# Start-up of a four-layer attention kernel: blank fills on VectorE, later weights loaded after the first rows, and a re-planned order

## The chip, the cores and the metric

The kernel runs on one core of one Trainium2 chip. The metric is the device time of one execution in microseconds (us); the median of seven executions is compared. Of the engines, PE is TensorE (matrix products), ACT is ScalarE, DVE is VectorE, POOL is GpSimd, and SP is SyncE, which here only issues DMA transfers. "PEld" are TensorE's weight loads.

## What is computed

Two kinds of layer alternate, A, B, A, B, over 2048 rows of 512 values, each added to its input:

```python
x = x + _A_ref(_layernorm(x, axis=-1), A_wqkv, A_wo)
x = x + _B_ref(_layernorm(x, axis=-1), B_wq, B_wk, B_wv, B_wo)
x = x + _A_ref(_layernorm(x, axis=-1), A_wqkv, A_wo)
x = x + _B_ref(_layernorm(x, axis=-1), B_wq, B_wk, B_wv, B_wo)
```

Layer A projects to q, k and v (32 heads of 16 values); each row attends to eight rows of its head, itself and every second one before it (offsets 0, 2, ..., 14), where they exist. Layer B has 32 query heads of 16 values on one shared k and v, and every row attends to all 2048 rows:

```python
scores = jnp.einsum("bhqd,bkd->bhqk", q, k) * (Dh ** -0.5)
p = _softmax(scores, axis=-1)
o = jnp.einsum("bhqk,bkd->bhqd", p, v)
```

## The kernel before

**Tiling.** The rows are split by parity and taken in four chunks of 512 rows (four tiles of 128). `chunk(l, c, ...)` does one chunk of a layer A: `ln` normalises, `qkv` projects, `unit` does banded attention, `a_out` projects back, and `b_in` normalises again and makes q, k and v of the following layer B. Layer B's attention is a stream of score tiles (`Stream`): a tile's exponential is either made on ScalarE, two tiles in one instruction (`pt`, L1486), or in a 16-bit approximation on VectorE (`t`, L1490) with a pass over four tiles on VectorE (`i`, L1500) and one on GpSimd (`i`, L1495). Such a tile costs three matmuls with the values, a ScalarE tile one (all `o`, L1512). Scores (`st`, `dv`, L1471) use a quarter of the array's rows each, and value products a quarter of its columns, so four of either run at once.

**What sets the order.** Nearly all instructions are emitted by a planner, `Sched`. Every piece of work is an `op` with a list of engines and assumed durations, its dependencies, a priority `prio` and an earliest start `after` (ns). The planner repeatedly takes the earliest candidate, weighs it by these constants, and writes down a fixed order for each engine; `chain` then ties each engine's instructions to that order. Each engine runs its list strictly in order. `SLACK`, `PATIENCE` and the table `BIAS` steer when the stream's scores are let in between other matmuls and which of the two ways a tile takes. Where the plan leaves TensorE idle, `keep_awake` adds idle matmuls against `zeros` (`stir`, L1079), reckoned at 108 ns for 256 columns; they go to a free bank of PSUM (named `stir` in the profile), or add zero to an open accumulation (`o<-zeros`). At the very start 46 such matmuls of 512 columns are emitted by hand.

**The start.** The work ahead of the planner is not ordered by it. SP loads x in five pieces (L1802: two of 256 KB, three of 512 KB), ScalarE's queue issues the four pieces of the q, k, v weights `w_sb` (L1806). Then SP issues `woA` (8 DMAs, the weights of the A output), `wq_sb` (4), `wk_sb`, `wv_sb` (one each) and `woB` (4), the weights of layer B. GpSimd builds the small constants: the identity, the band mask's pattern (L889 to L895, made into bits by VectorE at L898), `halves`, `off`, `kmask` (L320 to L324) and `sel` (L1831). After these it clears what must be zero or one: the check buffers (L850), the padding in the v tiles of both buffer sets (`v`, `lb`, `KAB`, L988), all of `k` (L989), `P` (L991), `vs` (L992), and layer B's value padding by `pad_v` (L1096 to L1098).

**The first rows.** `ln` takes statistics on VectorE (L1156), combines them (L1162), lets GpSimd work out scale and shift in four small instructions (L1166 to L1169), for rows 0, 1 and then 2, 3 in the first two chunks, and normalises on any of three engines (L1184, L1187). In these two chunks TensorE transposes the result (`pT`, L1198); in others a DMA does. Then come the projections (L1135).

Of the kernel before, what the change touches and what calls it, by code (L numbers as in the profile page):

```python
# [435 lines left out]
SLACK, PATIENCE = 1158.8, 464.8  # L436
# [180 lines left out]
class Stream:  # L617

    GROUP = 4
    BIAS = {"act": -72.8, "act2": 4311.9, "vec": 438.1, "pv": 169.4, "pv_in": 209.6, "batch": 19, "few": 15.0,  # L620
            "copy": 1.4, "pass": 284.2, "lag": -654.7, "both": 628.5, "next": 1451.0, "late": 32.5, "open": 55.9,
            "close": 6.0}
# [216 lines left out]
class Checks:  # L839
# [4 lines left out]
    def __init__(self, nc, pool):  # L844
        self.nc, self.pool = nc, pool
        self.a = pool.tile([128, 256], F32, name="chk_a")
        self.b = pool.tile([128, 2, 32], F32, name="chk_b")
        self.t = None
        for x in (self.a, self.b):
            nc.gpsimd.memset(x[:], 0.0)  # L850
# [36 lines left out]
def build_band_mask(nc, cpool):  # L887
# [10 lines left out]
    nc.vector.tensor_scalar(out=bits[:].bitcast(I16), in0=m[:], scalar1=-1.0, scalar2=None, op0=ALU.mult)  # L898
# [42 lines left out]
class Net:  # L941

    PRIO, LATER = 0.0, -201.0

    def __init__(self, ctx, tc, w, S, nlayers, out_view):
        self.tc, self.nc, self.w, self.out_view = tc, tc.nc, w, out_view
        nc = tc.nc
# [38 lines left out]
        for k2 in range(4):  # L986
            for B in self.sets:
                nc.gpsimd.memset(B.vpair(k2)[:, :, :, :, DH:2 * DH], 0.0)  # L988
        nc.gpsimd.memset(self.k.t[:], 0.0)  # L989
        for b in self.P.bufs:  # L990
            nc.gpsimd.memset(b.t[:], 0.0)  # L991
        nc.gpsimd.memset(self.vs.t[:, :, :, DH:2 * DH], 0.0)  # L992
        self.pad_v(0)
# [15 lines left out]
        self.tail, self.first_pass = {}, {}  # L1009
# [83 lines left out]
    def pad_v(self, l):  # L1093
        va, vd = self.va[l], self.vd[l]
        g = self.nc.gpsimd
        out = [g.memset(va[:, :, 17:32], 0.0), g.memset(va[:, :, 16:17], 1.0), g.memset(vd[:, :, :, 17:32], 0.0)]  # L1096
        for j in range(NJ):
            out.append(g.memset(vd[:, :, j, 16:17], J_W[j]))  # L1098
        return out
# [25 lines left out]
    def mm_full(self, pairs, deps, name):  # L1125
# [17 lines left out]
        b = self.op("pe", half * MM, rest, behind=[a], solid=True, prio=-1760.9 + self.PRIO)  # L1143
# [3 lines left out]
    def ln(self, B, src, deps, after=(0.0,) * 4, quick=False, own=None):  # L1147
# [6 lines left out]
        for i in range(4):  # L1154
            def emit(op, i=i):
                self.chain("dve", nc.vector.bn_stats(out=stats[:, i, :], in_=src(i)))  # L1156

            st.append(sm.used(self.op("dve", 596.0, emit, [*deps[i], *sm.prev], prio=-73.4 + self.PRIO, after=after[i])))
# [13 lines left out]
        for some in ((0, 1), (2, 3)) if quick else ((0, 1, 2, 3),):  # L1172
            ag = sm.used(self.op("dve", 70.0 * len(some), lambda op, some=some: aggr(op, some), [st[i] for i in some],
                                 prio=-1530.5 + self.PRIO))
            ag = sm.used(self.op("pool", 1700.0, lambda op, some=some: scalars(op, some), [ag], prio=10.4 + self.PRIO))
            nm.update(dict.fromkeys(some, ag))
        B.xnT.renew()
        xnT, done = B.xnT.t, []
        for i in range(4):
            xn = ring.next()  # L1180

            def norm(op, i=i, xn=xn):
# [3 lines left out]
                else:  # L1186
# [5 lines left out]
                                        prio=146.4 + self.PRIO, port=("pool",))))  # L1192
            cols = xnT[:, :, i * 128:(i + 1) * 128]
            if quick:
                def turn(op, xn=xn):
                    pT = self.psum(op, [128, 4, 128], BF16, "pT")
                    for ft in range(4):
# [4 lines left out]
                                     prio=-1811.6 + self.PRIO))  # L1202
                tr = self.op({"act": act_ns(512), "dve": 400.0}, 0, lambda op, cols=cols, tr=tr: self.chain(
                    op.eng, (nc.scalar.copy if op.eng == "act" else nc.vector.tensor_copy)(
                        out=cols, in_=self.y.pop(tr)[:])), [tr], frees=[tr], prio=125.9 + self.PRIO)
            else:
                tr = xn.used(self.op("sp", 1300.0, lambda op, cols=cols, xn=xn: self.chain(
                    "sp", nc.sync.dma_start_transpose(out=cols, in_=xn.t[:])), [n, *B.xnT.prev], prio=-2414.9 + self.PRIO))
# [9 lines left out]
    def chunk(self, l, c, deps):  # L1218
# [5 lines left out]
        after = ((7300.0, 7300.0, 8800.0, 8800.0) if c == 0 else (9000.0 + 2500.0 * c,) * 4) if first else (0.0,) * 4  # L1224
# [33 lines left out]
    def qkv(self, B, c, xops, quick):  # L1258
# [20 lines left out]
        def split(op):  # L1279
            for g in range(4):  # L1280
                for h in range(2):
# [5 lines left out]
        k = kp if quick else [[B.k.used(B.oncA.used(self.op("sp", 8 * DMA, split, [*kp, *B.k.prev],  # L1287
                                                                  prio=-248.9 + self.PRIO)))]] * 4
# [3 lines left out]
        for k2 in range(4):  # L1292
# [13 lines left out]
            m0 = self.op("pe", 450.0, mm, xops + vb.prev, want=("bank", "aux"), solid=True, mode="h64", prio=1077.4 + self.PRIO)  # L1306
            m = self.op("pe", 450.0, lambda op, mm=mm: mm(op, i=1), behind=[m0], solid=True, mode="h64", prio=-515.0 + self.PRIO)
# [21 lines left out]
    def unit(self, B, c, t, kd, qkv):  # L1329
# [14 lines left out]
        for gh in range(2):  # L1344
            def score(op, gh=gh):
                st = self.st[op] = self.slot[op.buf].tile([128, 2, 512], F32, name="st")
                for col, w, kx, _, q0 in parts:
                    for j in range(2):
# [7 lines left out]
                         solid=True, mode="row", prio=-259.7 + self.PRIO)  # L1356
            exps.append(P.used(self.op("act", act_ns(2 * ncol), lambda op, gh=gh, sc=sc: self.chain(
                "act", nc.scalar.activation(out=P.t[:, gh, :, c0:UC], in_=self.st.pop(sc)[:, :, c0:UC], func=AF.Exp,  # L1358
                                            scale=DH ** -0.5)), [sc], frees=[sc], prio=-46.0 + self.PRIO)))
# [8 lines left out]
        ms = P.used(self.op("dve", 800.0, mask, exps, prio=-532.6 + self.PRIO, port=("dve",)))  # L1368
# [16 lines left out]
        def dn(op):  # L1385
            o = state["o"]
            for gh in range(2):
                for q0, q1, b1 in ((SPILL, NQ, 0), (0, SPILL, 0 if over else 1)):
                    for j in range(2):
# [9 lines left out]
                     prio=193.1 + self.PRIO, want=("bank", "aux"))  # L1399
        p1 = self.op("pe", 165.0, lambda op: pv(op, 1), behind=[p0], solid=True, mode="c64", prio=-2353.3 + self.PRIO)  # L1400
        m = self.op("pe", 250.0, dn, behind=[p1], solid=True, mode="c64", prio=-1347.9 + self.PRIO)
        m.lend = p0
        for x in (p0, p1, m):
# [5 lines left out]
            out=lg.t[:], in_=state["o"][:, 1, :], func=AF.Ln)), [m, *lg.prev], prio=-177.0 + self.PRIO))  # L1409
        ex = lg.used(rc.used(self.op("act", act_ns(256), lambda op: self.chain("act", nc.scalar.activation(  # L1410
            out=rc.t[:], in_=lg.t[:], func=AF.Exp, scale=-1.0)), [ln, *rc.prev], prio=-60.7 + self.PRIO)))
        if t == 0 and kd == 0:
# [3 lines left out]
            [ex, *B.oncA.prev], frees=[m], prio=-246.0 + self.PRIO)))  # L1416
# [6 lines left out]
        lg.used(self.op("pool", 1400.0, see, [ex], prio=1614.3, port=("pool",)))  # L1423
        return on

    def a_out(self, B, l, c, units):
        nc, adds = self.nc, []
        for qi in range(4):
# [7 lines left out]
                prio=-22.5 + self.PRIO))  # L1436
        return adds

    def b_in(self, B, l, c, adds):
# [3 lines left out]
        m = self.proj(B, lambda kt: w.wkR[:, kt, :], xops, "kb")  # L1443
# [14 lines left out]
        v = B.xnT.used(self.op("pe", 400.0, mm, xops + self.padded[l], want=("bank", "aux"), solid=True, prio=209.4 + self.PRIO))  # L1458
# [56 lines left out]
    def close(self, n, bank, when):  # L1515
# [15 lines left out]
        e = X.used(self.op("dve", 599.0, evac, X.prev if fresh else list(X.cur), after=when, frees=[held], prio=-214.6))  # L1531
# [7 lines left out]
    def rows(self, l, qc, t, a, evac):  # L1539
# [43 lines left out]
        r = R2.used(S2.used(self.op("dve", 260.0, recip, [m, self.ready[l, qc, t, 0], *R2.prev], prio=-175.2)))  # L1583
        R2.used(S2.used(self.op("pool", 620.0, see, [r], prio=178.2)))
        d = R2.used(self.op("sp", 2 * DMA, to_dram, [r]))
        b = lb.used(self.op("sp", DMA, spread, [d, *lb.prev]))
        if t == 0:
            self.oncB.renew()
        self.ready[l, qc, t] = self.oncB.used(lb.used(X0.used(
            self.op("pool", 1300.0, scale, [b, m, *self.oncB.prev], prio=1009.5, port=("pool",)))))  # L1590
# [7 lines left out]
    def out_rows(self, l, qc, qi):  # L1598
        m = self.oncB.used(self.mm_full([(self.oncB.t[:, t, qi * 128:(qi + 1) * 128], self.w.woB[:, t, :])
                                         for t in range(4)], [self.ready[l, qc, t] for t in range(4)], "y"))  # L1600
        return self.op("dve", 599.0, lambda op: self.add_y(l, qc, qi, self.y.pop(m)[:]), [m], frees=[m], prio=-57.3)

    def retire_w(self):
# [7 lines left out]
        z = self.op("pool", 960.0, lambda op: self.chain("pool", nc.gpsimd.memset(w.woP, 0.0)), done, prio=661.6)  # L1611

        def load(op):
            for g in range(4):
# [5 lines left out]
                             self.oncA.cur, prio=4790.1)  # L1620
# [14 lines left out]
    def close_tail(self, a, evac):  # L1635
# [6 lines left out]
        for cs in parts:  # L1642
# [7 lines left out]
            dns.append(self.op("pe", 4 * MM * n / 512, mm, [evac], want=("bank", "aux"), solid=True, prio=FIRST))  # L1650
# [54 lines left out]

    def run(self):
        self.padded = {0: []}
        adds = []
        for c in range(self.NQC):
            adds += self.chunk(0, c, [[]] * 4)  # L1710

        def pad(op):
            for l in range(1, self.NB):
                for i in self.pad_v(l):
                    self.chain("pool", i)

        self.padded[1] = [self.op("pool", 1500.0, pad, adds, prio=-258.1)]
        warm = self.bank[0].tile([128, 512], F32, name="stir", tag="bk")
        for _ in range(46):
# [48 lines left out]
def kernel(  # L1768
# [30 lines left out]
    last = None  # L1799
    pieces = [(0, 2), (2, 2), (4, 4), (8, 4), (12, 4)]  # L1800
    for n, (t0, k) in enumerate(pieces):
        i = nc.sync.dma_start(out=x_bf[:, t0:t0 + k, :], in_=xv[t0 // 8, :, t0 % 8:t0 % 8 + k, :])  # L1802
        order_after(tc, i, last)
        last = i
        if n < 4:
            nc.scalar.dma_start(out=w.w_sb[:, n, :], in_=wqv[:, n, :])  # L1806
    w.zeros = cpool.tile([128, 128], BF16, name="zeros")
    nc.vector.memset(w.zeros[:], 0.0)  # L1808
    w.ident = build_ident(nc, cpool)
    w.nhalf = cpool.tile([128, 4], F32, name="nhalf")  # L1810
    nc.gpsimd.memset(w.nhalf[:], -0.5)
    w.band = build_band_mask(nc, cpool)
    w.halves = build_halves(nc, cpool)
    w.off = {j: cpool.tile([128, 4], I32, name=f"off{j}") for j in (1, 2)}
    for j in (1, 2):
        nc.gpsimd.memset(w.off[j][:].bitcast(I16), round(J_OFF[j]))
    nc.scalar.preload_act_table_set("natural_log_exp_and_others")
    wov = A_wo.rearrange("(t h g d) n -> g h d t n", t=4, h=2, g=4, d=DH)
    for g in range(4):
        for h in range(2):  # L1820
            nc.sync.dma_start(out=w.woA[32 * g + 16 * h:32 * g + 16 * h + 16, :, :], in_=wov[g, h])
    w.wq_sb = load_w(nc, cpool, B_wq, "wq_sb", D, (nc.sync,))
    bconsts = build_consts_B(nc, cpool, B_wk, B_wv)
    w.wv_sb, w.wkR, w.kmask = bconsts
    w.woB = load_w(nc, cpool, B_wo, "woB_sb", D, (nc.sync,))
    w.wo_dram = B_wo
    w.kscale = fpool.tile([128, 2], F32, name="kscale")
    nc.vector.tensor_scalar(out=w.kscale[:], in0=w.kmask[:], scalar1=K_SCALE, scalar2=None, op0=ALU.mult)

    w.sel = fpool.tile([128, 128], F32, name="sel")  # L1830
    nc.gpsimd.memset(w.sel[:], 1.0)  # L1831
    nc.gpsimd.affine_select(out=w.sel[:].rearrange("p (g r) -> p g r", r=32), in_=w.sel[:].rearrange(
        "p (g r) -> p g r", r=32), compare_op=ALU.is_equal, fill=0.0, base=-16, pattern=[[-32, 4], [0, 32]],
        channel_multiplier=1)
# [38 lines left out]
```

## Time and profile before

| | us |
|---|---|
| seven runs, median (lowest to highest) | 1540.32 (1536.35 to 1546.76) |
| the profiled execution, its own time | 1546.78 |
| its span in the trace | 1545.1 |
| busy in the span: PE / ACT / DVE / POOL | 1493.1 / 1449.1 / 1341.1 / 889.4 |
| first 16 us: busy PE / DVE / ACT / POOL | 12.60 / 8.67 / 1.28 / 14.44 |
| mean granted TensorE clock over the span | 0.977 |

A timeline line of the profile reads: start, time covered, engine, line of the program, operation, what is written from what, shape, count; in square brackets the engine's idle time before it and what ended it. A matmul row that is long is not PE at its peak, since matmuls are pipelined. The chain of waits is the path of work followed back from the last instruction, each step to what released it. The granted clock is the share of TensorE's full clock.

The profiled execution's own time is 1.7 us more than its span. Changes are worked out against it and then set against the median, which is 6.5 us lower.

### The profile page before, as it was taken

Reading aid. Unit: us, or ns where it says so; the run is one execution under the profiler, and the core shown is the slowest. Engines: PE = TensorE matmul, PEld = TensorE weight load, DVE = VectorE, ACT = ScalarE, POOL = GpSimd, SP = SyncE. Lnnn points to the kernel's source line nnn. Section 1 sums busy time; section 2 is a strip of 40 time slices with the busy share of each in tenths; the row PEclk is TensorE's granted clock in tenths of the full one; section 3 lists DMA queues with packets and bytes.
Section 4 is the critical chain, followed back from the end, with each engine's and each line's share of the span. In section 5 each row is a group of like instructions: output and inputs, shape, how many; then the busy total and the mean of one; then the engine's idle time right before and its main releaser. Section 6 shows DMA issues by size and latency. Waiting matters only on the chain.

```text
span 1545.1 us, 42500 instructions
## 1 busy us (share of the span) xinstructions
PE 1493.1 (97%) x17361; PEld 519.1 (34%) x17361; DVE 1341.1 (87%) x2261; ACT 1449.1 (94%) x1769; POOL 889.4 (58%) x749
## 2 busy tenths in 40 slices
PE   8999999999999999999999999999999999999997
PEld 3544334322333224323243233422332223223322
DVE  5585875899689996999879997899999999999996
ACT  4788997899999998999999999999999999999995
POOL 5553633566465654656565664756666656665664
PEclk8999996999999999999999999999999999999998
DMA  4001110011110011100111001001000000000000
GB/s 137 4 15 16 16 29 3 15 39 27 22 21 19 13 22 21 27 13 13 25 20 23 13 13 28 3 19 38 26 13 13 13 26 13 13 13 29 15 13 16
DMA packets 84114, 32.95 MB, mean 21 GB/s; under 512 B 71688, under 2 KB 77448, under 8 KB 83912
## 3 DMA queue, kind: packets, MB, share of 16 engines
q1 hardware_dynamic: 83048, 28.33, 8.6%
q8 instruction: 138, 2.26, 0.6%
q10 hardware_dynamic: 864, 1.84, 0.3%
q14 instruction: 64, 0.52, 0.1%
HBM read 13.53 MB, written 2.61 MB: 10 GB/s over the span
## 4 chain that ended last, share of the span: by engine, by line
PE 61%; ACT 27%; issue 5%; DVE 4%; POOL 1%; SPq 1%; DMA 1%; ACTq 0%; DVEq 0%; POOLq 0%
ACT pt L1486 24%; PE o L1512 23%; PE st L1471 19%; PE y L1135 3%; PE stir L1079 2%; PE qb L1135 2%; PE k L1135 2%; PE q L1135 2%; PE v L1302 2%; DVE t L1490 2%; PE dv L1471 2%; ACT P L1358 1%; PE st L1351 1%; PE oa L1378 1%; SPq L1283 1%
## 5 line engine op out<-in xcount | busy, mean ns | idle before, releaser
L1486 ACT ACTIVATE pt<-st 128x1024 bf16<-128x1024 f32 x1368 | 1281.3, 1151 | 22.6 <-PE dv L1471 9.5
L1495 POOL TENSOR_TENSOR i<-t,off 128x1024 int32<-128x1024 int32 (+1 forms) x341 | 643.2, 1886 | 512.3 <-DVE i L1500 304.6
L1490 DVE TENSOR_SCALAR t<-dv 128x512 int16<-128x512 f32 x1360 | 868.9, 684 | 51.3 <-PE dv L1471 42.5
L1471 PE MATMUL st<-QT,KAB 32*128 32x512 bf16 x1403 | 276.9, 386 | 7.4 <-ACT pt L1486 4.9
L1512 PE MATMUL o<-pt,region 128*32 128x512 bf16 x1333 | 270.6, 388 | 0.6 <-DVE x_sb L1434 0.6
L1471 PE MATMUL st<-QT,region 32*128 32x512 bf16 x1333 | 261.2, 381 | 10.1 <-ACT pt L1486 7.1
L1512 PE MATMUL o<-pt,VEa 128*32 128x512 bf16 x1403 | 266.9, 392 | 0.6 <-ACT pt L1486 0.2
L1512 PE MATMUL o<-i,region 128*32 128x512 f16 x1430 | 254.7, 387 | 0.6 <-DVE i L1500 0.4
L1500 DVE TENSOR_SCALAR i<-t 128x2048 int16<-128x2048 int16 (+1 forms) x341 | 239.1, 701 | 0.5
L1512 PE MATMUL o<-i,VEd 128*32 128x512 f16 x1290 | 232.3, 390 | 0.8 <-POOL i L1495 0.7
L1471 PE MATMUL dv<-QT,region 32*128 32x512 bf16 x715 | 230.2, 385 | 0.8 <-DVE t L1490 0.6
L1471 PE MATMUL dv<-QT,KAB 32*128 32x512 bf16 x645 | 204.3, 386 | 0.7 <-DVE t L1490 0.7
L1512 PE MATMUL o<-t,region 128*32 128x512 f16 x715 | 187.4, 387 | 0.0
L1471 PEld LDWEIGHTS <-KAB 32*128 32x128 bf16 x2048 | 90.7, 91 | 267.6 <-issue 263.3
L1471 PEld LDWEIGHTS <-region 32*128 32x128 bf16 x2048 | 93.1, 91 | 260.2 <-issue 257.2
L1512 PE MATMUL o<-t,VEd 128*32 128x512 f16 x645 | 167.1, 388 | 0.0
L1512 PEld LDWEIGHTS <-region 128*32 128x32 f16 (+1 forms) x3478 | 77.9, 94 | 162.2 <-issue 157.9
L1358 ACT ACTIVATE P<-st 128x576 bf16<-128x576 f32 (+1 forms) x128 | 88.8, 717 | 5.9 <-PE st L1351 4.1
L1512 PEld LDWEIGHTS <-VEd 128*32 128x32 f16 x1935 | 66.8, 94 | 74.6 <-issue 69.9
L1512 PEld LDWEIGHTS <-VEa 128*32 128x32 bf16 x1403 | 59.8, 94 | 82.3 <-issue 80.3
L1365 DVE TENSOR_TENSOR P<-P,bandmask 128x576 int32<-128x576 int32 x64 | 54.8, 858 | 30.9 <-ACT P L1358 28.6
L1079 PE MATMUL stir<-zeros 32*128 32x256 bf16 (+11 forms) x267 | 72.3, 300 | 8.5 <-DVE zeros L1808 1.1
(176 smaller groups left out, 1245.3 us busy)
## 6 DMA issues: line engine op xcount, KB each, us to landing
lb<-rd SPq DMA_DIRECT2D x31, 256.0 KB
X<-X SPq DMA_DIRECT2D x124, 32.0 KB
k<-oncA SPq DMA_DIRECT2D x48, 64.0 KB
w_sb<-in_A_wqkv_dram ACTq DMA_DIRECT2D x4, 384.0 KB
region<-in_A_x_dram SPq DMA_DIRECT2D x3, 512.0 KB
out_dram<-w_sb SPq DMA_DIRECT2D x3, 512.0 KB
S<-X SPq DMA_DIRECT2D x62, 8.0 KB
rd<-R SPq DMA_DIRECT2D x62, 8.0 KB
```

Source lines behind the costliest of these rows:

```text
L1079: self.chain("pe", self.nc.tensor.matmul(out[0:m, 0:n], lhsT=z[0:k, 0:m], rhs=z[0:k, 0:1].to_broadcast([k, n]), start=start, stop=start, t ...
L1135: self.chain("pe", self.nc.tensor.matmul(st["ps"][:], lhsT=lhsT, rhs=rhs, start=first and n == 0, stop=last and n == len(some) - 1))
L1283: self.chain("sp", nc.sync.dma_start(out=B.k.t[r, :, :, h, :], in_=B.oncA.t[r].rearrange("p t (b i) -> p t b i", i=64)))
L1302: self.chain("pe", nc.tensor.matmul(ps[0][64 * a:64 * a + 64, i], lhsT=B.xnT.t[:, kt, kb * 64:(kb + 1) * 64], rhs=wv[:, kt, a, :, :], star ...
L1358: "act", nc.scalar.activation(out=P.t[:, gh, :, c0:UC], in_=self.st.pop(sc)[:, :, c0:UC], func=AF.Exp, scale=DH ** -0.5)), [sc], frees=[sc ...
L1365: self.chain("dve", nc.vector.tensor_tensor(out=x, in0=x, in1=self.w.band[:].unsqueeze(1).to_broadcast([128, 16, NQ // 2]), op=ALU.bitwise ...
L1471: self.chain("pe", self.nc.tensor.matmul(out, lhsT=self.KAB[l][32 * g:32 * g + 32, a, kt * 128:(kt + 1) * 128], rhs=self.QT[32 * g:32 * g ...
L1486: self.chain("act", self.nc.scalar.activation(out=self.pt[pt][:, 0:n, :], in_=self.st.pop(key)[:, 0:n, :], func=AF.Exp, scale=E_SCALE))
L1490: self.chain("dve", self.nc.vector.tensor_scalar(out=self.t[buf][:, r, :].bitcast(I16), in0=self.dv[bank][:], scalar1=-U_BIAS, scalar2=U_B ...
L1495: i = self.nc.gpsimd.tensor_tensor(out=self.i[out][:, 0:n, :].bitcast(I32), in0=self.t[buf][:, 0:n, :].bitcast(I32), in1=self.w.off[j][:, ...
L1500: i = self.nc.vector.tensor_scalar(out=self.i[out][:, 0:n, :].bitcast(I16), in0=self.t[buf][:, 0:n, :].bitcast(I16), scalar1=J_OFF[j], sca ...
L1512: self.chain("pe", self.nc.tensor.matmul(self.o[bank][32 * g:32 * g + 32, :], lhsT=lhsT, rhs=rhs, start=first, stop=last, tile_position=(0 ...
```

## The change

Fills: `Checks`, `Net.__init__` and `pad_v(0)` clear on VectorE in place of GpSimd, before the first statistics, in the order check buffers, P, v padding, vs, layer B's value padding. `k` is not cleared any more. `kmask` is made on VectorE, `kscale` straight after it; the band mask's bits are made on GpSimd. `nhalf` comes ahead of the identity on GpSimd.

Loads: only the first three x pieces are issued at once. `late_loads` gives the planner a one-element VectorE memset (earliest 8400 ns) that writes into `woA`, and SP's remaining 20 DMAs wait for it: `woA`, `wq_sb`, `wk_sb`, `wv_sb`, the last two x pieces, `woB`. `wkR` (VectorE) and `sel` (GpSimd) are planned from 26,000 and 30,000 ns.

Plan: the planner is told that VectorE, GpSimd and TensorE are free at 4500, 4000 and 8300 ns; 17 idle matmuls instead of 46 open TensorE; the earliest starts of the first statistics move from 7300 and 8800 to 4800 and 7100 ns; `SLACK`, `PATIENCE`, `BIAS` and most priorities get new values (a few are shown), so that the order of all engines differs through the whole run.

```diff
-SLACK, PATIENCE = 1158.8, 464.8
+SLACK, PATIENCE = 658.9, 588.4
-    BIAS = {"act": -72.8, "act2": 4311.9, "vec": 438.1, "pv": 169.4, "pv_in": 209.6, "batch": 19, "few": 15.0,
-            "copy": 1.4, "pass": 284.2, "lag": -654.7, "both": 628.5, "next": 1451.0, "late": 32.5, "open": 55.9,
-            "close": 6.0}
+    BIAS = {"act": -51.1, "act2": 3433.0, "vec": 438.1, "pv": 169.4, "pv_in": 208.5, "batch": 22, "few": 15.0,
+            "copy": 1.8, "pass": 108.5, "lag": -2240.5, "both": 721.7, "next": 104.9, "late": 31.8, "open": 55.9,
+            "close": 4.0}
...
-        for x in (self.a, self.b):
-            nc.gpsimd.memset(x[:], 0.0)
+        self.blank = [nc.vector.memset(x[:], 0.0) for x in (self.a, self.b)]
...
-    nc.vector.tensor_scalar(out=bits[:].bitcast(I16), in0=m[:], scalar1=-1.0, scalar2=None, op0=ALU.mult)
+    nc.gpsimd.tensor_scalar(out=bits[:].bitcast(I16), in0=m[:], scalar1=-1.0, scalar2=None, op0=ALU.mult)
...
-        for k2 in range(4):
-            for B in self.sets:
-                nc.gpsimd.memset(B.vpair(k2)[:, :, :, :, DH:2 * DH], 0.0)
-        nc.gpsimd.memset(self.k.t[:], 0.0)
-        for b in self.P.bufs:
-            nc.gpsimd.memset(b.t[:], 0.0)
-        nc.gpsimd.memset(self.vs.t[:, :, :, DH:2 * DH], 0.0)
-        self.pad_v(0)
+        v = nc.vector
+        blank = [*self.checks.blank, *(v.memset(b.t[:], 0.0) for b in self.P.bufs),
+                 *(v.memset(B.vpair(k2)[:, :, :, :, DH:2 * DH], 0.0) for B in self.sets for k2 in range(4)),
+                 v.memset(self.vs.t[:, :, :, DH:2 * DH], 0.0), *self.pad_v(0, v)]
+        for i in blank:
+            self.chain("dve", i)
...
-        after = ((7300.0, 7300.0, 8800.0, 8800.0) if c == 0 else (9000.0 + 2500.0 * c,) * 4) if first else (0.0,) * 4
+        after = ((4800.0, 4800.0, 7100.0, 7100.0) if c == 0 else (8000.0 + 3000.0 * c * c,) * 4) if first else (0.0,) * 4
...
-        k = kp if quick else [[B.k.used(B.oncA.used(self.op("sp", 8 * DMA, split, [*kp, *B.k.prev],
-                                                                  prio=-248.9 + self.PRIO)))]] * 4
+        k = kp if quick else [[B.k.used(B.oncA.used(self.op("sp", 8 * 720.0, split, [*kp, *B.k.prev],
+                                                                  prio=90.5 + self.PRIO)))]] * 4
...
+    def late_loads(self):
+        nc, w = self.nc, self.w
+        hold = self.op("dve", 70.0, lambda op: self.chain("dve", nc.vector.memset(w.woA[:, 0, 0:1], 0.0)), after=8400.0,
+                       prio=FIRST)
+
+        def load(op):
+            for out, in_ in w.late:
+                self.chain("sp", nc.sync.dma_start(out=out, in_=in_))
+
+        self.op("sp", DMA * len(w.late), load, [hold])
...
+        S = self.sched
+        S.now.update(dve=4500.0, pool=4000.0, pe=8300.0)
+        S.mode, S.end, S.array_busy = "full", 8300.0, [(4000.0, 8300.0)]
+        self.late_loads()
...
-        for _ in range(46):
+        for _ in range(17):
             self.idle_matmul(warm, (128, 128), 512, True)
...
+    for _, o, i in pieces[:3]:
+        then("sp", nc.sync.dma_start(out=o, in_=i))
+    for k in range(4):
+        nc.scalar.dma_start(out=w.w_sb[:, k, :], in_=wqv[:, k, :])
...
+    then("dve", nc.vector.memset(w.zeros[:], 0.0))
+    for h in range(2):
+        then("dve", nc.vector.memset(w.kmask[:, h:h + 1], float(h)))
+        for g in range(4):
+            then("dve", nc.vector.memset(w.kmask[32 * g:32 * g + 16, h:h + 1], float(1 - h)))
+    then("dve", nc.vector.tensor_scalar(out=w.kscale[:], in0=w.kmask[:], scalar1=K_SCALE, scalar2=None, op0=ALU.mult))
...
+    w.late = [(w.woA[32 * g + 16 * h:32 * g + 16 * h + 16, :, :], wov[g, h]) for g in range(4) for h in range(2)]
+    w.late += [(w.wq_sb[:, k, :], rows(B_wq)[:, k, :]) for k in range(4)]
+    w.late += [(w.wk_sb[:], rows(B_wk)), (w.wv_sb[:], rows(B_wv))]
+    w.late += [p[1:] for p in pieces[3:]]
+    w.late += [(w.woB[:, k, :], rows(B_wo)[:, k, :]) for k in range(4)]
```

## The prediction

> **What bounds the kernel now.** I read the page from the top: engine shares, then the chain of waits, then the timeline of the first 40 us, because there the diff moves most.
>
> ```profile
> span 1545.1 us, 42500 instructions
> PE 1493.1 (97%) x17361; PEld 519.1 (34%) x17361; DVE 1341.1 (87%) x2261; ACT 1449.1 (94%) x1769; POOL 889.4 (58%) x749
> ...
> PE 61%; ACT 27%; issue 5%; DVE 4%; POOL 1%; SPq 1%; DMA 1%; ACTq 0%; DVEq 0%; POOLq 0%
> ```
>
> Nearly all of the 1545 us is TensorE and ScalarE handing work to each other; GpSimd is 1% of the chain. So what the front can give is a few us, and the rest of the effect must come from the re-planned body. The front, from the timeline (start, duration, instruction):
>
> ```profile
> 4.79 1.29 DVE L1156 BATCH_NORM_STATS2 sm<-region 128x6 f32<-128x512 bf16 x2 [3.79 <-DMA region<-in_A_x_dram]
> ...
> 8.46 5.63 DVE L898 TENSOR_SCALAR bandmask<-bandones 128x72 int16<-128x72 bf16 x1
> 8.52 5.58 DVE L1828 TENSOR_SCALAR kscale<-kmask 128x2 f32<-128x2 f32 x1
> 10.89 2.06 POOL L991 MEMSET P<- 128x1152 bf16 x2
> ...
> 14.46 0.25 POOL L1166 TENSOR_SCALAR sm<-sm 128x2 f32<-128x2 f32 x1
> ...
> 16.64 1.03 PE L1198 MATMUL pT<-ident,xn 128*128 128x128 bf16 x8 [2.98 <-DVE xn L1187]
> ...
> 17.46 2.98 PE L1079 MATMUL stir<-zeros 128*128 128x256 bf16 x7
> ...
> 20.50 1.01 PE L1198 MATMUL pT<-ident,xn 128*128 128x128 bf16 x8
> ...
> 22.30 1.87 PE L1135 MATMUL q<-xnT,w_sb 128*128 128x512 bf16 x4
> ```
>
> Row statistics are ready at 6.3, but the scalars of the first two rows begin on GpSimd at 14.46, behind its fills. Eight us later the first projection starts, at 22.30. Between stand seven idle matmuls (`stir`) of 2.98 us, 0.43 each.
>
> Granted clock, by windows (columns: window, length, busy PE, PEld, DVE, ACT, POOL with counts, clock, DMA share, GB/s):
>
> ```profile
> 18.00:20.00 2.00, 1.78 (x5) 0.47 (x5) 2.00 (x6) 0.35 (x1) 1.06 (x2) 0.50 0.78 158
> ...
> 24.00:26.00 2.00, 2.00 (x6) 0.70 (x5) 0.09 (x1) 1.30 (x2) 0.06 (x1) 0.50 0.00 0
> ...
> 28.00:30.00 2.00, 2.00 (x31) 1.23 (x30) 2.00 (x5) 1.87 (x5) 0.00 (x0) 1.00 0.00 0
> ```
>
> The first projections run at half clock.
>
> **Fills moved to VectorE.** GpSimd loses 14.36 - 4.7 us of fills. That includes one of 3.5 us on k, dropped outright: both evacuations of k write all of it through the mask. VectorE gets 10 small memsets on kmask, the two-element kscale, and 19 fills of 3584 elements in sum (chk 320, P 2x576 words, v/lb/KAB 8x128 words, vs 64, VEa 256, VEd 768). No VectorE fill of this size is in the trace. The nearest rows: two statistics of 512 elements start 0.61 apart, two aggregates of 6 start 0.12 apart, the zeros fill of 64 words took 0.11; about 0.06 + 1.04 ns per element. That makes 19 x 0.06 + 3584 x 1.04 ns = 4.9. Start 0.89, zeros to 1.0, kmask to 1.7, kscale 0.5, fills: end near **7.1**.
>
> *Rule against row.* The Trainium skill, "SBUF — State Buffer", § Who interferes with whom: a VectorE instruction with at most one SBUF input outside the two-port modes never contends with GpSimd; a tensor_scalar in a two-port mode waits until the GpSimd instruction under way has ended. By it the fills are free and kscale waits 0.3 at most. The row speaks against the change: L898, a tensor_scalar, stood 5.63 us, through the k fill, both P fills and the V pads. If kscale likewise waits for GpSimd's first true pause, now about 4.3, the fills end at 9.2. Before 4 us GpSimd's rows stall for their own results (chain pauses of 0.05 at 1.96, 2.41, 2.90), in the stretch of L898 hardly. I take 0.5, with +2.1 as the far end.
>
> Rows 0 to 3 have landed by 7.04 (the statistics started then on their arrival), so the fills, not the rows, are now late. Statistics and aggregates (1.2 + 0.25) to 8.5; scalars 8.65 to 10.35 (1.67 before, 14.46 to 16.13); ScalarE norm 0.81, GpSimd norm 0.90; first transposes near 11.3 instead of 16.64, **5.3 earlier**. Bandmask goes to GpSimd ahead of all this and costs about 0.2 by 4.3, hidden.
>
> **What is late next: the idle matmuls.** In the built program's order 16 stirs, not 7, stand between the first and second transpose pair, and 4, not 2, before q. Each waits for the one before: starts lie 0.428 apart at half clock and 0.328 at full, where the planner counts 0.108. Pair one ends at 11.9; 16 x 0.428 = 6.85 gives 18.8; transposes 0.7; 4 x 0.43; q at about **21.3**: only 1.0 earlier. At full clock: 11.9 + 5.25 + 0.5 + 1.3 = 18.9, 3.4 earlier, and q, k, q save another 2.2 (1.87 + 1.71 + 1.25 against 3 x 0.86).
>
> *Second rule.* "TensorE: Matmul & The Clock Gate", § Why this matters for your kernels: no idle gaps above about 3 us, or an idle window halves the clock. With 17 warm-ups ending at about 7.4 (12 x 0.427 + 5 x 0.218 after 1.06, as in the trace) instead of 46 ending at 13.66, the gap grows from 2.98 to 3.9. By the rule the change would itself cause the half clock; by the row a gap of 2.98 already did, so nothing more is lost. I take the row: half clock, -1.0. The rule's free-running window leaves a real chance of full clock.
>
> **Loads moved behind the rows.** SP issues three x pieces, then waits for a one-element memset on VectorE between the statistics of rows 2 and 3, about 8.5. Behind it stand 20 DMAs: 8 woA, 4 wq, wk, wv, two x pieces, 4 woB. The woA issues took 9.76 before, 5.2 of it waits on earlier transfers; I use 0.7 each (the 64 KB pieces k<-oncA took 0.61 to 0.78): 5.6, wq 1.85, wk and wv 0.94, so the x pieces are issued near 17.5 and, at about 4 to 5 us of flight (0.81 to 4.76 for the first), land by 23. They are wanted after the first q and k evacuations; those statistics ran at 27.56. If that cover went, VectorE would stand with the first band mask queued behind. woA is first used at 58.75, wq and kb at 86: covered. The memset is 0.07 on VectorE, hidden. w_sb gains nothing: it landed before q was ready.
>
> wkR and sel move to 26 and 30 by plan, inside gaps.
>
> **The re-planned body.** New constants reorder everything. From the two programs' order: exponentials of two tiles 1368 to 1358 (+1 single), t copies 1360 to 1379, passes 341 to 345 on VectorE and on GpSimd, PV matmuls 6816 to 6854, own-bank stirs after the start 212 to 172, filler into o 123 to 107. I price each by its share of the chain of waits, divided by its count:
> - stir 2.1% of 1545 = 32.4 us, less 2.5 in the first 30 us: 0.141 each; 40 fewer: -5.6. Bounds: 0, and 40 x 0.22 = -8.8 (all of 0.328 beyond the plan's 0.108).
> - pt 23.7% = 366 us / 1368 = 0.27; 9.5 fewer: -2.5.
> - PV 22.9% = 354 us / 6816 = 0.052; 38 more: +2.0.
> - t 1.8% = 28 us / 1360 = 0.02; 19 more: +0.4.
>
> Sum -5.7. The passes and o fillers lie beside other work; without that cover the passes would cost 4 x 0.70.
>
> **Sum.** -1.0 - 5.7 = -6.7. The profiled execution took 1546.8 (span 1545.1 and 1.7 around it) and would take 1540.1. It stands 6.5 above the median of the runs, 1540.3, so the forecast for the median is **1533.6**.
>
> **Rivals.**
> - *The start stays at full clock.* For it: the window's phase is chance. Against: a gap of 3.9. q 3.4 earlier and 2.2 faster: -5.6 - 5.7, **1529**.
> - *The body's gain is hidden*: with fewer fillers PE simply waits longer for ScalarE, busy 94%. For it: pt carries 29 to 35% of the chain after 800 us. Only the start counts: **1539.3**. If kscale also starves (+2.1), 1541.4.
> - *The change does not do what it says*: the stirs eat all of the 5.3. That is most of my forecast's start already; with the body it gives 1534.6.
> - *The clock falls asleep*, the one that ends slower. Fillers hold the clock; 56 fewer are placed. Twice the clock missing from 1.00, summed over 6-us windows, gives before about 65 us at half clock, the longest stretch near 245 to 265. Each half-clock us costs up to 0.5 of PE work. From 14 us more the forecast gain is gone; with 24 us more it is +12 - 6.7, **1545.6**. Against: fewer fillers because less idle is planned.
>
> **How the numbers follow.** Forecast 0.60, full clock at the start 0.22, hidden body or starved fills 0.11, clock 0.07. Range: down from 1533.6 by 4.6 (start at full clock), 3.2 (stirs at their upper price) and 3.4 (four windows of half clock less) to 1522; up by 5.6 (stirs worth nothing) and 2.1 (starved kscale) to 1542. A measurement tells about 0.3% from no change, so faster means below 1535.7 and slower above 1544.9. The forecast's case spreads some 4 us, so nine tenths of it and the full-clock case are faster: 0.54 + 0.22, and a little of the others: 0.78. Slower 0.06, the rest 0.16.
>
> **What would show it.** Scalars near 8.7 and transposes near 11.3: fills right. kscale far above 0.5: the row was right, not the rule. q at 21 with 16 stirs of 0.43 before it: the stir step; q at 19 and clock 1.00: the rival. Chain share of stir down to about 1.7%, pt a little down: the body. Half-clock time far above 65 us, or the statistics of the third chunk waiting on DMA region, would make the forecast wrong.

## The result, and the profile after

| us | before | changed |
|---|---|---|
| median | 1537.32 (35 runs, 1531.64 to 1546.76) | 1530.60 (14 runs, 1523.16 to 1535.02) |
| profiled execution, own time | 1546.78 | 1532.6 |
| its span | 1545.1 | 1530.9 |

The ratio is 0.9954, 95% interval 0.9938 to 0.9969: faster by about 7 us. A repeat on another occasion gave 0.9973 (0.9958 to 0.9988), so some 4 to 7 us, 5.6 in the mean of the two. That is close to the forecast -6.7, but the experiments below show that its terms were not right: a gain well above the expected one and a loss that was not forecast are in it. The profiled execution of before is its slowest on record, so the two profiles differ by more than the medians.

The page of the changed kernel, the same lines as before:

```profile
span 1530.9 us, 42419 instructions
PE 1470.1 (96%) x17325; PEld 505.4 (33%) x17325; DVE 1351.1 (88%) x2314; ACT 1440.0 (94%) x1756; POOL 886.2 (58%) x727
...
PE 53%; ACT 33%; DVE 8%; issue 6%; POOL 0%; ACTq 0%; DVEq 0%; POOLq 0%
```

GpSimd, 1% of the chain before, has left it. ScalarE's busy time fell by 9.1 us, though its share of the chain grew from 27 to 33%. Now the start, from the timeline:

```profile
1.96 0.17 DVE L1844 TENSOR_SCALAR kscale<-kmask 128x2 f32<-128x2 f32 x1
...
2.54 1.15 DVE L987 MEMSET P<- 128x576 uint32 x2
...
5.94 0.67 DVE L1153 BATCH_NORM_STATS2 sm<-region 128x6 f32<-128x512 bf16 x1
...
7.51 0.24 POOL L1163 TENSOR_SCALAR sm<-sm 128x2 f32<-128x2 f32 x1 [3.18 <-DVE sm L1159]
...
10.06 0.62 PE L1195 MATMUL pT<-ident,xn 128*128 128x128 bf16 x8 [3.78 <-POOL xn L1184]
...
10.52 6.66 PE L1077 MATMUL stir<-zeros 128*128 128x256 bf16 x16
...
17.24 1.01 PE L1195 MATMUL pT<-ident,xn 128*128 128x128 bf16 x8
...
18.04 1.70 PE L1077 MATMUL stir<-zeros 128*128 128x256 bf16 x4
19.89 1.86 PE L1132 MATMUL q<-xnT,w_sb 128*128 128x512 bf16 x4
```

The first scalars begin 7.0 us earlier (14.46 to 7.51) and the first transposes 6.6 earlier, but q only 2.4 earlier: 16 idle matmuls, 0.42 each, stand in between, while the inputs of the second transposes were normalised by 12.6. Windows of 2 us, columns as in the prediction (the eighth number is the granted clock), just before q, at the end of the half clock and behind it:

```profile
18.00:20.00 2.00, 1.68 (x8) 0.54 (x6) 0.00 (x0) 0.93 (x2) 0.00 (x0) 0.50 1.03 334
24.00:26.00 2.00, 1.66 (x15) 0.94 (x13) 1.01 (x3) 1.14 (x3) 0.00 (x0) 0.91 0.00 0
28.00:30.00 2.00, 2.00 (x10) 0.78 (x8) 1.58 (x4) 2.00 (x5) 0.00 (x0) 1.00 0.00 0
```

q runs at half clock again, and full clock comes back at 24.3 instead of 26.5. So far everything went nearly as forecast.

### The profile page after: what moved, and what is told of

It is laid out like the page before. It is cut to its first block, busy times and chain, and to the rows that moved or that the text cites. A ratio compares the mean times of both kernels' runs of the same rounds, so it can differ in the third digit from the quotient of the medians.

```text
span 1530.9 us, 42419 instructions
## 1 busy us (share of the span) xinstructions
PE 1470.1 (96%) x17325; PEld 505.4 (33%) x17325; DVE 1351.1 (88%) x2314; ACT 1440.0 (94%) x1756; POOL 886.2 (58%) x727
## 3 DMA queue, kind: packets, MB, share of 16 engines
q8 instruction: 137, 2.24, 0.6%
## 4 chain that ended last, share of the span: by engine, by line
PE 53%; ACT 33%; DVE 8%; issue 6%; POOL 0%; ACTq 0%; DVEq 0%; POOLq 0%
ACT pt L1483 29%; PE o L1509 19%; PE st L1468 17%; DVE t L1487 3%; PE y L1132 3%; PE q L1132 2%; PE stir L1077 2%; PE dv L1468 2%; PE k L1132 2%; ACT P L1355 2%; PE qb L1132 2%; PE v L1299 1%; PE st L1348 1%; PE oa L1375 1%; ACT logs L1405 1%
## 5 line engine op out<-in xcount | busy, mean ns | idle before, releaser
L1492 POOL TENSOR_TENSOR i<-t,off 128x1024 int32<-128x1024 int32 x345 | 652.5, 1892 | 507.4 <-DVE i L1497 339.7
L1487 DVE TENSOR_SCALAR t<-dv 128x512 int16<-128x512 f32 x1379 | 879.3, 686 | 53.4 <-PE dv L1468 49.6
L1468 PE MATMUL st<-QT,KAB 32*128 32x512 bf16 x1383 | 271.5, 384 | 10.9 <-ACT pt L1483 7.9
L1497 DVE TENSOR_SCALAR i<-t 128x2048 int16<-128x2048 int16 x345 | 240.9, 699 | 1.1 <-PE o L1509 0.2
L1509 PE MATMUL o<-i,VEd 128*32 128x512 f16 x1330 | 241.8, 388 | 0.0
L1468 PE MATMUL dv<-QT,KAB 32*128 32x512 bf16 x665 | 213.4, 383 | 1.0 <-DVE t L1487 0.9
L1509 PE MATMUL o<-t,region 128*32 128x512 f16 x714 | 181.9, 385 | 1.2 <-DVE t L1487 1.2
L1509 PE MATMUL o<-t,VEd 128*32 128x512 f16 x665 | 173.1, 386 | 0.8 <-DVE t L1487 0.7
L1416 POOL TENSOR_TENSOR logs<-logs 128x256 f32<-128x256 f32 x64 | 44.6, 697 | 57.8 <-ACT rec L1407 57.8
```

Of the source, the lines that this page charges most:

```text
L1416: self.chain("pool", nc.gpsimd.tensor_tensor(out=lg.t[:], in0=lg.t[:], in1=lg.t[:], op=ALU.mult))
L1468: self.chain("pe", self.nc.tensor.matmul(out, lhsT=self.KAB[l][32 * g:32 * g + 32, a, kt * 128:(kt + 1) * 128], rhs=self.QT[32 * g:32 * g ...
L1487: self.chain("dve", self.nc.vector.tensor_scalar(out=self.t[buf][:, r, :].bitcast(I16), in0=self.dv[bank][:], scalar1=-U_BIAS, scalar2=U_B ...
L1492: i = self.nc.gpsimd.tensor_tensor(out=self.i[out][:, 0:n, :].bitcast(I32), in0=self.t[buf][:, 0:n, :].bitcast(I32), in1=self.w.off[j][:, ...
L1497: i = self.nc.vector.tensor_scalar(out=self.i[out][:, 0:n, :].bitcast(I16), in0=self.t[buf][:, 0:n, :].bitcast(I16), scalar1=J_OFF[j], sca ...
L1509: self.chain("pe", self.nc.tensor.matmul(self.o[bank][32 * g:32 * g + 32, :], lhsT=lhsT, rhs=rhs, start=first, stop=last, tile_position=(0 ...
```

## The experiments

Every ratio is against the kernel before, run beside it on the same chip; 0.1% is about 1.5 us.

**Start and plan apart.** With the planner's constants go the counts of the body: the new start with the old constants has before's counts (1368 exponentials of two tiles; after q 212 idle matmuls into a bank of their own, `stir`, called own-bank below), the old start with the new constants has the changed kernel's. The order is not quite the same: ScalarE's instructions in plan_only differ from the changed kernel's at 450 of some 1750 places.

```diff
 # front_only: the changed kernel, with before's constants
-SLACK, PATIENCE = 658.9, 588.4
+SLACK, PATIENCE = 1158.8, 464.8
...
 # plan_only: before, with the changed kernel's constants
-SLACK, PATIENCE = 1158.8, 464.8
+SLACK, PATIENCE = 658.9, 588.4
...
```

> The new start with every planner constant of before; the planned body is that of before in its counts (1368 pt, 212 own-bank stirs, 6816 value products). Theory (start worth about 1 us, new plan about 5.7): 0.9993 of before. Rival (the start is the whole gain): 0.9956. q begins near 20, as in the changed kernel, under both.

> The start of before with the changed kernel's planner constants; planned body counts as in the changed kernel (1358 pt, 172 own-bank stirs, 6854 value products). Theory: 0.9963 of before (-5.7 us), q near 22.3. Rival (the start is the whole gain): 1.000.

Measured: front_only 0.9983 (0.9972 to 0.9995), plan_only 0.9928 (0.9909 to 0.9948). The start is a small gain and the plan a large one, as the theory had it; but the plan alone gains about 11 us and the sum of both would be 0.991. Together they give 0.9954 to 0.9973, 4 to 7 us behind the plan alone and 7 to 9 behind the sum. Something is lost when they meet.

Both were repeated beside each other, unchanged:

> The changed kernel once more, beside the next ones on one chip. If the half-clock stretches fall by chance of the window's phase, its list of them differs from the first profile's (236 to 250 gone or elsewhere) and the time is 0.995 again. If they belong to the order, the list is the same.

> Start of before with the new plan, a second time. If new start and new plan really spoil each other: 0.993 again, below the changed kernel beside it. If the first difference was chance: both near 0.994.

Measured: 0.9973 (0.9958 to 0.9988) and 0.9931 (0.9911 to 0.9951). The loss is real. In the profiles the changed kernel leads plan_only by 5 us at its first layer-B score (95.7 against 100.5) and is behind later. In between lies a half-clock stretch from 236 to 250, near 238 to 249 in the repeat, that neither profile of plan_only has.

The mean granted clock of every execution is on record, profiled or not, so its time at half clock can be worked out: twice the share missing from 1.00, times the span. Within one kernel, one us more of it goes with 0.33 us more of time (fitted over 210 executions, correlation 0.96). The last column takes each kernel's mean time to 50 us of half clock with this slope; it is an estimate, but it parts what an order is worth from what the clock does to it (before comes to 1538.9 to 1539.3 on each of four occasions). The kernels not yet named are those of the sections below:

| kernel (executions) | us at half clock, mean (lowest to highest) | time at 50 us of it |
|---|---|---|
| before (84) | 46 (31 to 62) | 1539.0 |
| front_only (22) | 49 (37 to 65) | 1534.4 |
| plan_only, both (12) | 43 (33 to 49) | 1528.5 |
| changed, both (38) | 64 (40 to 89) | 1527.9 |
| pad18 (6) | 49 (43 to 58) | 1526.7 |
| fills_back (14) | 70 (40 to 96) | 1532.9 |
| no_start_stirs (6) | 41 (30 to 58) | 1522.8 |
| warm28_no_stirs (6) | 41 (24 to 73) | 1524.3 |
| nss_pad20 (6) | 60 (40 to 80) | 1524.4 |
| no_body_stirs (5) | 54 (42 to 67) | 1515.7 |
| no_stirs (5) | 44 (30 to 57) | 1512.3 |
| front_no_stirs (6) | 63 (49 to 76) | 1519.0 |

The changed kernel has 21 us more at half clock than plan_only, about 7 us of time: all that it lags behind. By order alone it is 11 us faster than before, and 18 us more at half clock take 6 of them back. (The profiled execution of before has 71 us at half clock, more than any of the 84, so its clock is not typical.)

**How far the start's delay reaches the end.**

```diff
 # fills_back: the changed kernel's order, fills on GpSimd
-        v = nc.vector
-        blank = [*self.checks.blank, ...
+        v = nc.gpsimd
+        blank = [v.memset(self.k.t[:], 0.0), *self.checks.blank, ...
...
-            self.chain("dve", i)
+            self.chain("pool", i)
```

> The changed kernel, planned order kept, with all the blank fills and the one of k put back on GpSimd ahead of the first scalars. Scalars near 14 instead of 7.5, q near 26. If a delay of the start reaches the end in full, 6 us worse than the changed kernel (0.9995 of before); if the body takes it up, 0.9956. My theory: in full.

Measured: 1.0015 (0.9994 to 1.0036), q at 26.5. The 6.6 us of delay at q are 8 at the end (0.5% against the mean of the two measurements of the changed kernel), or 5 at equal half clock: the body has little slack that hides a late start.

**The idle matmuls before q.**

```diff
 # no_start_stirs: none planned before 17 us
-        if gap < 60.0 or self.mode is None:
+        if gap < 60.0 or self.mode is None or until < 17000.0:
             return
```

> The changed kernel without the 20 idle matmuls between the first transposes and q, all else in the same order. Theory (each costs 0.43 in series and q waits for them): q near 14.5 to 15 instead of 19.9, 5 us better than the changed kernel, 0.9923 of before. Rival (the clock stays low for longer without them, or the body does not use an earlier start): 0.9956.

Measured: 0.9891 (0.9865 to 0.9916), 10 to 13 us better than the changed kernel (against its two measurements). TensorE's timeline of it:

```profile
10.07 0.62 PE L1195 MATMUL pT<-ident,xn 128*128 128x128 bf16 x8 [3.47 <-POOL xn L1184]
12.23 1.03 PE L1195 MATMUL pT<-ident,xn 128*128 128x128 bf16 x8 [1.54 <-DVE xn L1184]
14.00 1.87 PE L1132 MATMUL q<-xnT,w_sb 128*128 128x512 bf16 x4 [0.73 <-ACT xnT L1201]
```

q starts at 14.00, 5.9 earlier, and at equal half clock 5 us of that are there at the end. The rest is less half clock, 41 us instead of 64; the stretch at 236 is gone here too.

Keeping TensorE busy up to the first transposes adds nothing that can be measured:

```diff
 # warm28_no_stirs: no_start_stirs with
-        for _ in range(17):
+        for _ in range(28):
```

> The changed kernel without the 20 idle matmuls before q, with 28 instead of 17 opening ones, so that TensorE idles under 1.5 us before the first transposes. Clock theory (the gap of 3.8 us halves the clock): full clock at q, some 2.4 us better than without the idle matmuls alone, 0.9875 of before. Rival (the window after the transposes is too idle anyway): half clock at q all the same, 0.989.

Measured: 0.9881 (0.9862 to 0.9901), not to be told from 0.9891. In its profile the clock is full until 13.2 and half for 3.4 us instead of 6.8, but q starts at 13.79 and runs at half clock all the same, as the rival had it.

**What starts the stretch at 236.** TensorE's timeline of the changed kernel just ahead of it:

```profile
234.43 0.23 PE L1077 MATMUL stir<-zeros 64*32 64x176 bf16 x1
234.59 0.24 PE L1348 MATMUL st<-q,k 32*128 32x72 bf16 x3
235.75 0.26 PE L1348 MATMUL st<-q,k 32*128 32x72 bf16 x7 [0.93 <-issue]
```

In the middle of a series of equal small matmuls, with nothing to wait for, TensorE halts (1.13 us from start to start). "issue" means the profile shows no cause. Counted through the trace (TensorE's matmuls and weight loads in order of time, each a record), the halt comes at TensorE's record 6848, in both profiles of the changed kernel and in fills_back; before's own profile has one of 0.75 us at the same record, at 244.4, where its longest half-clock stretch begins. All such halts without a wait in the other profiles (records 1984, 2240, 2496, 2752, 15040, 20160, 24000, where few records are missing ahead of them) also lie at 192 plus a multiple of 256. The page's transfers of kind "instruction" on queue q8, 137 of 2.24 MB in all, are 16 KB each. The Trainium skill, "Runtime: NRT & Kernel Launch", § Instruction fetch mechanics, says that an engine's program is streamed in blocks of 16 KiB, 256 instructions, and that the crossing is mostly hidden. In this stage, some 150 matmuls and as many weight loads in 4 us, it is not always.

The trace also has the start and end of each of these transfers. The block before the halt begins at 232.34; a transfer runs from 233.41 to 234.48; TensorE, through with the block's 256 instructions after 2.29 us, goes on at 235.75, which is 1.27 us after the landing. It is so at every halt of more than 0.35 us without a wait, 27 in all 14 profiles: TensorE goes on 1.23 to 1.60 us after such a transfer has landed. An arbitrary instant between 40 and 260 us lies so behind a landing in 5% of cases. So the halt is a wait for the program. Where no records are missing, 2.9 to 3.7 us pass from the beginning of a block to the end of the halt behind it; a block that TensorE goes through sooner than that can end in a halt.

Whether a block ends in a dense place depends on how many instructions stand ahead of it. The changed kernel has 37 idle matmuls before q, plan_only 55, no_start_stirs 17. So the place alone can be moved:

```diff
 # pad18: the changed kernel; nss_pad20: no_start_stirs, with 20
         for _ in range(17):
             self.idle_matmul(warm, (128, 128), 512, True)
+        for _ in range(18):
+            self.idle_matmul(warm, (128, 128), 16, True)
```

> The changed kernel with 18 more idle matmuls of 16 columns after the 17 opening ones, in TensorE's idle time before the first transposes; nothing else moves, but all of TensorE's program stands 36 instructions later, where it stands in the kernel with only the new plan. Fetch theory (the 1.1 us halt at TensorE record 6848, a multiple of 256 past the first 192, starts the half-clock stretch at 236): no halt near 236, that stretch gone, 4 to 5 us better than the changed kernel, 0.992 of before. Rival (the loss belongs to the earlier start itself): 0.9954 to 0.9973 as the changed kernel.

> The kernel without the 20 idle matmuls before q, with 20 of 16 columns put in after the opening ones: its start, but the changed kernel's place of every later TensorE instruction in the program. Fetch theory: the halt is back near 230, with a half-clock stretch after it, 4 to 5 us worse than without the padding, 0.9915. Rival (the place does not matter): 0.989.

Measured: pad18 0.9921 (0.9903 to 0.9939), nss_pad20 0.9921 (0.9894 to 0.9949). Both as the fetch theory had it: 18 matmuls that do nothing and are hidden in an idle time make the changed kernel 5 to 8 us faster (against its two measurements), and 20 of them make no_start_stirs 4.6 us slower. The intervals touch the changed kernel's first one and overlap in the second case; what carries the conclusion is that both moves went the forecast way by the forecast size, and that the time at half clock moved with them (64 to 49 us, and 41 to 60). Another padding that leaves the place as it was, by 128 matmuls, was not run. Windows of the changed kernel (first) and of pad18, columns as in the prediction:

```profile
232.00:236.00 4.00, 2.92 (x150) 2.11 (x147) 3.27 (x6) 3.48 (x7) 1.85 (x3) 1.00 0.02 4
236.00:240.00 4.00, 3.94 (x29) 1.02 (x25) 2.41 (x5) 3.35 (x5) 2.33 (x3) 0.50 0.02 4
240.00:244.00 4.00, 3.94 (x138) 2.76 (x138) 1.01 (x3) 3.10 (x6) 2.49 (x2) 0.50 0.01 4
```

```profile
232.00:236.00 4.00, 3.85 (x157) 2.14 (x155) 3.29 (x6) 4.00 (x8) 1.34 (x2) 1.00 0.02 4
236.00:240.00 4.00, 3.67 (x87) 1.58 (x81) 2.74 (x5) 4.00 (x9) 3.46 (x4) 1.00 0.02 4
240.00:244.00 4.00, 3.89 (x157) 2.40 (x139) 3.02 (x5) 4.00 (x10) 2.41 (x2) 1.00 0.01 4
```

With the halt, busy TensorE falls to 2.92 of 4 us, and the clock is half in the next windows; ScalarE, fully busy in pad18, starves (3.35, 3.10). And nss_pad20 at the same instruction of its program:

```profile
234.00 0.24 PE L1348 MATMUL st<-q,k 32*128 32x72 bf16 x4
235.07 0.24 PE L1348 MATMUL st<-q,k 32*128 32x72 bf16 x6 [0.84 <-issue]
```

The halt is back; half clock follows from 237.5 to 258. The halt alone does not decide: no_start_stirs and warm28_no_stirs stop at the same block end for 0.36 and 0.39 us from start to start, the first with no loss of clock, the second with half clock from 232 to 249; no_body_stirs has half clock there, from 232 to 245, without a halt. The stage is near the edge. All five profiles with a long halt in it went over; but of nss_pad20's six executions three have 40 to 49 us at half clock and three 70 to 80, so that a halt makes the loss likely, not certain. In other stages halts as long (1.04 us at 71.95 in pad18) passed without it.

**The idle matmuls of the body.**

```diff
 # no_body_stirs: until > 17000.0 leaves out those after q; no_stirs: all
+        return
         gap = until - self.end - SWITCH - 20.0
```

> The changed kernel without any idle matmul after q (172 own-bank, 107 into o), same order. By the price of the chain of waits (0.14 each): 24 us better, about 0.98 of before. By the rival that the clock falls asleep without them: half-clock time well above 65 us, and slower than the changed kernel, above 0.9954.

> The changed kernel with the 17 opening idle matmuls and no other. If the gains of leaving out those before q (1.0 to 1.1%... 0.9891 against 0.9963) and those of the body (0.9858) add: 0.979. If without both the clock falls asleep: half-clock time well above 75 us and no better than 0.9858.

Measured: no_body_stirs 0.9858 (0.9836 to 0.9880), no_stirs 0.982 (0.9799 to 0.9841; median 1510.25). The two gains do not quite add (0.979 forecast), but the clock does not fall asleep: no_stirs has 44 us at half clock in the mean, against 64 in the changed kernel and 46 in before. The page of no_stirs:

```profile
span 1506.2 us, 41765 instructions
PE 1422.8 (94%) x16970; PEld 489.5 (33%) x17026; DVE 1352.3 (90%) x2314; ACT 1437.7 (95%) x1756; POOL 888.3 (59%) x727
...
PEclk9998999999999999999999999999999999999998
```

This is the fastest kernel of the study, about 28 us ahead of before and 20 of the changed one, from a one-line edit. The price is below my 0.141 each: from no_start_stirs to no_stirs, 0.7%, 11 us for 172 own-bank stirs and 107 into o, 0.06 per own-bank stir if those into o cost nothing; from the changed kernel to no_body_stirs 16 us, of which 12 at equal half clock.

**Where the plan's gain comes from.**

```diff
 # front_no_stirs: front_only with the same return
+        return
         gap = until - self.end - SWITCH - 20.0
```

> The new start with before's planner constants and no idle matmul but the 17 opening ones: the partner of the changed kernel without them (0.982). If the new plan's gain is that it places fewer idle matmuls, as my body term has it (the rest of that term is -0.1 us), both meet: 0.982. If the new plan gains by its order itself, this one is worse by most of the plan's 10 us: 0.987 to 0.989. A halt for instructions in a dense stage would add some 4 us to either.

Measured: 0.990 (0.9884 to 0.9917), against 0.982 for its partner. Without any planned idle matmul the new plan is still 12 us ahead: its gain is not only that it places fewer. But the clock has a share in the 12: front_no_stirs has 63 us at half clock, no_stirs 44. At equal half clock 6.7 us are left; between front_only and the changed kernel it is 6.5, on the old start (before and plan_only) 10.5. Left-out idle matmuls also cost clock here: front_only has 49 us at half clock.

The counts point to ScalarE's exponentials, 1359 rows instead of 1368, 9.5 full ones fewer. From the pages of front_no_stirs and no_stirs:

```profile
L1484 ACT ACTIVATE pt<-st 128x1024 bf16<-128x1024 f32 x1368 | 1280.8, 1154 | 19.1 <-PE dv L1469 7.8
L1484 ACT ACTIVATE pt<-st 128x1024 bf16<-128x1024 f32 x1359 | 1270.6, 1162 | 12.6 <-PE dv L1469 5.3
```

At their whole duration of 1.154 us they would be worth 11.0 us, more than the 6.5 to 6.7. The last stage, after the last `kb` projection, where only the stream of layer B runs, gives a price with the clock nearly equal: front_only has 546 exponentials there and lasts 524.8 us, the changed kernel 542 and 521.9 (7.9 and 8.1 us at half clock); front_no_stirs 546 and 525.1, no_stirs 542 and 522.2 (9.3 and 7.9). Four fewer for 2.9 us, about 0.7 each. (Before and plan_only differ by 5.8 us there, but before's profile has 13.3 us at half clock, plan_only's 7.5.) This is a match of counts and times, and other work differs with the counts; the split between the two ways of making a tile was not varied alone.

## Why the prediction was right, point by point

- **Fills to VectorE: right, priced slightly too high.** Forecast to end at 7.1, statistics began at 5.94. 19 fills took 3.8 us and not 4.9: P's 1.15 for 2 x 576 words is 1.0 ns per word, with hardly a fixed part. First transposes at 10.06 (forecast 11.3).
- **Rule against row: the rule held.** kscale took 0.17, the far end (+2.1) was never near. The row of 5.63 fits GpSimd's unbroken run of fills, which the change removed; no run here puts the two side by side again. VectorE's fills ran beside GpSimd's constants without a sign of waiting.
- **The stirs between the transposes: right.** 16 in 6.66 us (forecast 6.85), four more in 1.70, half clock, q at 19.9 (21.3).
- **Idle gap and clock: right.** The gap was 3.78 (3.9), q ran at half clock. The rival of a full-clock start did not happen. That the gap is the cause is not shown: with it closed (warm28_no_stirs) q ran at half clock too.
- **The loads: hidden, as forecast.** SP issued the x pieces at 14.72 (17.5): eight woA issues took 3.70, not 5.6, since nothing was ahead of them.
- **The start, -1.0: right in size on the new plan.** There, with TensorE's program at the same place, pad18 against plan_only, it is about -1 (0.9921 against 0.9928 and 0.9931), which is inside the intervals. On the old plan it is -2.6 (0.9983), -4.6 at equal half clock.
- **The body, -5.7: too small, and wrong inside.** It is -10.6 to -11 on the old start (plan_only), on the new one -6.5 at equal half clock. The term that failed is the exponentials, "0.27; 9.5 fewer: -2.5": a share of the chain of waits divided by the count. The last stage gives about 0.7 us for one, up to 1.15 would fit plan_only. With it failed the rest of the body, all that is not `stir`, put at -0.1: without planned idle matmuls in either kernel it is -6.7 at equal half clock. Why the share is too small is not shown; a second path that ends just behind the chain would do it. The stir term, -5.6, was too high: at 0.06 each it is about -2.4.
- **Not in the forecast at all: the halt for instructions** and the half clock behind it, worth 5 to 8 us against the changed kernel (pad18). It made up for what the body gained beyond its -5.7. So the forecast's sum met the median by errors of opposite sign, which is luck.
- **The slow rival (the clock falls asleep) did not happen as described.** no_stirs, which has no planned idle matmuls, has no more half clock than before (44 us, 46). But the changed kernel did get 18 us more of it, for another reason, and it took back 0.33 us for each, not the "up to 0.5" of the prediction.

## What to carry to other kernels

Do not take a share of the chain divided by the count for the price of one instruction: here it gave 0.27 us for an exponential that was worth about 0.7, with 1.15 of duration as the upper bound. Idle matmuls that wait on each other take their own latency (0.43 us at half, 0.33 at full clock) and not their columns: before putting them into a plan, run it once without any. When two edits that gain alone lose together, set the granted clock of all executions beside their times, look for a halt with no cause in a dense stage, and move the program by a few instructions before blaming either edit.

## What the runs showed of the hardware that was not expected

- TensorE can halt for 0.5 to 1.4 us (start to start) at the end of a 256-instruction block (record 192 + 256 n) when it has gone through the block in 2.2 to 2.7 us. Where the block took 2.84 to 2.94, the halt was 0.36 to 0.39. Nothing but "issue" marks it. That it is a wait for the program is shown by the transfers: 27 of 27 halts end 1.23 to 1.60 us after one has landed. That the place in the program decides is shown by pad18 and nss_pad20.
- One such halt of 0.75 to 1.4 us is followed by 10 to 20 us of half clock in every profile that has it in that stage (before, the changed kernel twice, fills_back, nss_pad20), though TensorE then shows as busy almost all the time. It is not followed by it in every stage.
- A kernel's executions differ mostly by their time at half clock: 0.33 us for each us of it, over 210 executions of 12 kernels (correlation 0.96).
- The clock was halved after an idle gap of 3.78 us, but also after one of 2.98 us (before), and in warm28_no_stirs at 13.2, where no gap since the first matmul is longer than 1.55 us. Every stretch of half clock ahead of the last is 3.4 us long or a multiple of it.
